# Halves of the FFN operands: powers of two moved into ScalarE's scale, GpSimd's multiplications taken out

## The chip, the cores and the metric

One Trainium2 chip, one of its cores. The time is device microseconds of one execution of the whole kernel; three runs of the kernel before have the median 1286.19 us (1284.73 to 1286.59).

## The reference

Eight sequences of 576 tokens with 8 heads of 64 go through a thresholded attention; its output is a matrix x of 4608 tokens by 512. After it comes the feed-forward part (FFN), the one that the change touches:

```
x = attn_out.transpose(0, 2, 1, 3).reshape(B * S, H * D)     # 4608 x 512
h = x @ w_in                                                 # w_in  512 x 2048
g = np.where(h > 0.0, h, np.exp(np.minimum(h, 0.0)) - 1.0)
out = g @ w_out                                              # w_out 2048 x 512
```

All is float32.

## The kernel before, in words

Most of the program runs attention and the FFN of earlier tokens side by side. There the two FFN products are done block-wise with fewer products (sums of blocks of the weights and tokens are made first, and the partial products are added up again). The last such products, "second_round" of the group before the last two, have their matmuls on L1818, their additions out of PSUM on VectorE at L1827, L1836 and L1838, further additions on GpSimd at L1831, and sums of g at L1765.

The last two groups of 512 tokens, called g7 and g8, are done in another way, which takes the span from 1086 us on (its halves are begun at about 1056 us): each operand is split in two halves of a shorter number format (F32R, which TensorE multiplies in one pass), and three products of halves take the place of one full float32 product. The token plane of 128 x 512 and the weight plane of 128 x 512 each become three planes:

- index 0, the **cut**: the operand times CUT, rounded on writing to F32R (ScalarE, L2004 for tokens, L2024 for weights)
- index 1, the **rest**: operand minus cut (VectorE; tokens at L2008 straight to F32R; weights at L2028 into a float32 slot, after which GpSimd multiplies it by 1/EPS = 4096 into F32R at L2031)
- index 2, the **cross** plane (VectorE; tokens at L2012, in-weights at L2035, out-weights at L2253, once for each token group)

The first round, for each group and each of 16 blocks f of the hidden width (32 units), is 8 matmuls of cut with cut and rest with rest (L2187), a scale by 1 + EPS of the bank in PSUM by ScalarE (L2191), and 4 matmuls of the cross planes two units later (L2200). Then follow exp on ScalarE (L2211), minus 1 on GpSimd (L2214) and the ELU's end on VectorE (L2217), which leaves the raw g block. The second round has, for each group and each f, 12 matmuls (L2264): three for each of four blocks of 128 tokens. EDGE = 3 blocks f at the beginning and at the end of a group are taken together, so that their planes are wanted together.

The order of the work is written by hand. `at(t, job)` puts a job into an agenda at a time of a made-up clock, and `on_pe(cost, job)` first issues all jobs that are due and then moves that clock on by the cost of the matmuls. The times say only in which order instructions go into the queues of the engines; on the chip each engine takes its queue in order and waits for what an instruction needs. A unit costs 2.73 of that clock. `issued(key, x)` pulls the agenda forward when a matmul needs a plane that is not issued yet.

Planes live in slots of 128 x 512. `take` gets one (a float32 or F32R slot that an old tile left, else one from the queue `free`, oldest first), and `drop` gives it back; whoever takes it later waits on the chip for its last reader. The float32 rest of a weight ("d") takes such a slot for a short while. The raw g blocks take float32 slots as well.

Of the kernel before, what the change touches and what calls it, by code (L numbers as in the profile page):

```python
# [10 lines left out]
FP32 = mybir.dt.float32  # L11
U32 = mybir.dt.uint32
I32 = mybir.dt.int32
F32R = mybir.dt.float32r
AF = mybir.ActivationFunctionType
ALU = mybir.AluOpType
# [352 lines left out]
def kernel(  # L369
# [10 lines left out]
    nc = tc.nc  # L380
# [3 lines left out]
    DM, DF = moe_w_in.shape  # L384
# [1230 lines left out]
    with tc.manual_schedule():  # L1615
# [11 lines left out]
        def at(t, f, key=None):  # L1627
            if key and stage[0]:
                t += MOVED.get(stage[0] + key, 0.0)
            serial[0] += 1  # L1630
            heapq.heappush(agenda, (t, serial[0], f))

        def until(t):
            while agenda and agenda[0][0] <= t:
                do_next()
# [333 lines left out]
        EDGE = 3  # L1969
        EPS, CUT = 2.0**-12, 1.0 - 2.0**-13  # L1970
        free, kept_for, parts, split_stack = deque(), {FP32: deque(), F32R: deque()}, {}, ExitStack()
# [9 lines left out]
        def slot(dt, wide=True):  # L1981
            if kept_for[dt]:
                t = kept_for[dt].popleft()
                return t, lambda: kept_for[dt].append(t)
            pool, name = home = free.popleft()
            return pool.tile([P, DM], dt, name=name), lambda: free.append(home)

        def drop(key, *which):
            for x in which or range(len(parts[key])):
                parts[key][x][1]()  # L1990
# [6 lines left out]
        def take(key, dt):  # L1997
            t = slot(dt)
            parts.setdefault(key, []).append(t)
            return t[0]  # L2000

        def cut(key, src, cols=slice(0, DM), fresh=True):
            a = take(key, F32R) if fresh else parts[key][0][0]
            nc.scalar.activation(a[:, cols], src()[:, cols], AF.Copy, scale=CUT)  # L2004

        def rest(key, src, cols=slice(0, DM), fresh=True):
            b = take(key, F32R) if fresh else parts[key][1][0]
            nc.vector.tensor_tensor(b[:, cols], src()[:, cols], parts[key][0][0].bitcast(FP32)[:, cols], ALU.subtract)  # L2008

        def cross(key, src, cols=slice(0, DM), fresh=True):  # L2010
            s = take(key, F32R) if fresh else parts[key][2][0]
            nc.vector.scalar_tensor_tensor(s[:, cols], parts[key][0][0].bitcast(FP32)[:, cols], 1.0 + EPS, src()[:, cols],  # L2012
                                           ALU.mult, ALU.subtract)

        def split_tokens(t, key, src, then=None):
            at(t, lambda: cut(key, src))
            at(t + 0.8, lambda: rest(key, src))
            at(t + 1.5, lambda: (cross(key, src), then and then()))

        def like(t, x):  # L2020
            return t.rearrange("p (j f) -> p j f", f=x.shape[2]) if len(x.shape) == 3 else t

        def weights_cut(key, src):
            nc.scalar.activation(like(take(key, F32R), src()), src(), AF.Copy, scale=CUT)  # L2024

        def weights_rest(key, src):
            d = take(("d", key), FP32)
            nc.vector.tensor_tensor(like(d, src()), src(), like(parts[key][0][0].bitcast(FP32), src()), ALU.subtract)  # L2028

        def weights_scaled(key):  # L2030
            nc.gpsimd.tensor_scalar(take(key, F32R), parts["d", key][0][0], 1.0 / EPS, None, ALU.mult)  # L2031

        def weights_cross(key):
            c, d = (parts[key][x][0].bitcast(FP32) for x in range(2))
            nc.vector.tensor_tensor(take(key, F32R), d, c, ALU.subtract)  # L2035

        def split_weights(t, key, src, then=None):
            at(t, lambda: weights_cut(key, src))
            at(t + 0.7, lambda: (weights_rest(key, src), then and then()))
            at(t + 1.4, lambda: (weights_scaled(key), drop(("d", key))))  # L2040
            if key[0] == "in":
                at(t + 2.1, lambda: weights_cross(key))

        def w_in_of(f):
            return lambda: w_in_at(slice(0, KJ), f * P, P)
# [1 line left out]
        def w_out_of(f):  # L2047
            return lambda: w_out_at(f, slice(0, DM))
# [10 lines left out]
        def x_of(g, j):  # L2059
            return lambda: xts[g][:, j]  # L2060
# [4 lines left out]
        def split_begin():  # L2065
            t = now[0]
            attending[0] = False
            attention.close()
            open_slots("r", 24, "right")
            xts[B] = xpool.tile([P, KJ, MAIN], FP32, name="xt")  # L2070
            nc.sync.dma_start(xts[B][:, : KJ - 1], xtail[: KJ - 1].rearrange("j p n -> p j n"))
            nc.sync.dma_start(xts[B][:, KJ - 1, : late_columns.start], xtail[KJ - 1, :, : late_columns.start])
            for f in range(EARLY_IN):
                at(t + 0.2 + 3.2 * f, lambda f=f: restore_in(f))
                split_weights(t + 0.6 + 3.2 * f, ("in", f), w_in_of(f))
            for j in range(KJ - 1):
                split_tokens(t + 2.2 + 3.2 * j, ("x", B - 1, j), x_of(B - 1, j))
            split_tokens(t + 12.0, ("x", B, 0), x_of(B, 0))
            for f in range(NU, NFT):
                at(t + 11.0 + 1.2 * (f - NU), lambda f=f: restore_in(f))  # L2080
# [3 lines left out]
        for pr in range(JOINED, NP + 2):  # L2084
            t = clock[0]
            b = pr // NPAIR
# [38 lines left out]
        g7, g8, last = B - 1, B, KJ - 1  # L2125
        for t, cols, fresh in ((clock[0] - 0.9, slice(CT, DM), True), (clock[0] + 0.4, slice(0, CT), False)):
            key = ("x", g7, last)
            at(t, lambda cols=cols, fresh=fresh: cut(key, x_of(g7, last), cols, fresh))
            at(t + 0.4, lambda cols=cols, fresh=fresh: rest(key, x_of(g7, last), cols, fresh))
            at(t + 0.8, lambda cols=cols, fresh=fresh: cross(key, x_of(g7, last), cols, fresh))  # L2130
        until(clock[0] + 0.3)
        run_extra(99)
        strassen.close()
# [22 lines left out]
        for j, t in ((1, 0.9), (2, 4.6), (last, 7.4)):  # L2156
            split_tokens(begin + t, ("x", g8, j), x_of(g8, j),
                         (lambda: [give(xpool, "xt", FP32) for _ in range(2)]) if j == last else None)
# [5 lines left out]
        def out_done(f):  # L2164
            if f % 4 == 3:
                give(const, f"w_out{f // 4}", F32R)

        for f in range(EARLY_IN, NFT):
            t = max(begin + 0.4 + 3.4 * (f - EARLY_IN), start_of[g7, f] - LEAD)
            if f < NU:  # L2170
                at(t - 0.5, lambda f=f: restore_in(f))
            split_weights(t, ("in", f), w_in_of(f), lambda f=f: in_done(f))
# [62 lines left out]
        def g_of(g, f):  # L2235
            def src():
                while (g, f) not in raw_g:
                    do_next()
                return raw_g[g, f]

            return src

        def start_f(t0, f):
            return t0 if f < EDGE else min(t0 + UNIT * f, t0 + UNIT * (NFT - EDGE))

        OUT_EARLY = 11
        for f in range(NFT):
            split_weights(begin + 22.0 + 3.9 * f if f < OUT_EARLY else start_f(middle, f) - 9.0, ("out", f), w_out_of(f),
                          lambda f=f: out_done(f))
            for g, t0 in ((g7, middle), (g8, end)):  # L2250
                t = start_f(t0, f) - (9.5 if f < EDGE else 6.0) + 2.9 * f * (f < EDGE)
                split_tokens(t, ("h", g, f), g_of(g, f), lambda g=g, f=f: drop(("g", g, f)))
                at(t + 2.2, lambda g=g, f=f: nc.vector.tensor_tensor(  # L2253
                    take(("cross", g, f), F32R), parts["out", f][1][0].bitcast(FP32), parts["out", f][0][0].bitcast(FP32),
                    ALU.subtract))

        left = {(g, f): 4 for g in (g7, g8) for f in range(NFT)}

# [79 lines left out]
```

## Time and profile before

| | |
|---|---|
| median of 3 runs | 1286.19 us |
| the profiled execution's own time | 1286.68 us |
| its span, first to last instruction | 1284.9 us |
| TensorE busy, matmuls | 1253.4 us (98% of the span) |
| VectorE / ScalarE / GpSimd busy | 1039.1 / 635.6 / 784.4 us |
| mean granted TensorE clock | 0.995 |
| first matmul of the first round (L2187) | at 1086.47 us of the span |
| first matmul of the second round (L2264) | at 1188.93 us |
| last matmul | ends by 1280.13 us |

How to read the profile: PE is TensorE's matmuls, PEld its weight loads, DVE VectorE, ACT ScalarE, POOL GpSimd. A group is "line engine operation out<-in": busy time, mean of one, then the idle time of the engine before it and what ended that ("<-"). In the table of stretches each engine has its busy time and number of instructions, then come the granted clock (1.00 is full) and the DMA engines' share. In the list in order of time a row is start, duration, engine, line, and in square brackets how long the engine had been idle and for whom. The tile names in it are those of memory that was used before under that name, since slots are handed on: "l" and "r" are the two pools of slots.

### The profile page before, as it was taken

To read this page: it belongs to the slowest core of one execution; us is meant where nothing else is said; L and a number is where in the kernel's file an instruction comes from. 1 tells how busy PE (TensorE), PEld (TensorE's weight loads), DVE (VectorE), ACT (ScalarE), POOL (GpSimd) and SP (SyncE) were. 2 spreads that over 40 slices of the span, in tenths; PEclk is the share of its full clock that TensorE was granted. 3 is DMA by queue.
4 is the path that set the end of the run, shared out by engine and by line. 5 is a ranking of instruction groups with operands and counts; after the bars stand their busy time and mean duration, and the time that the engine had idled before them with its cause. 6 is when DMAs were issued, how large, how long until landed. Compare 5 with 4: busy or idle time off the path is not lost. (4 is left out here: it accounts for less than half of the span.)

```text
span 1284.9 us, 21199 instructions
## 1 busy us (share of the span) xinstructions
PE 1253.4 (98%) x6598; PEld 959.7 (75%) x6598; DVE 1039.1 (81%) x2199; ACT 635.6 (49%) x1331; POOL 784.4 (61%) x1093
## 2 busy tenths in 40 slices
PE   8999999999999999999999999999999998989998
PEld 6675575467778887878788888788788886767876
DVE  6888877878889979898889888988899767645775
ACT  7899775664443535252625353434435342535322
POOL 4778655776586747684767567665767463575110
PEclk9999999999999999999999999999999999989999
DMA  7566689998989988999889898989899871000001
GB/s 139 150 171 189 172 235 250 259 255 201 243 228 237 251 238 228 266 246 233 239 230 260 221 257 223 252 232 237 221 243 244 257 220 56 1 1 1 1 33 33
DMA packets 325551, 245.74 MB, mean 191 GB/s; under 512 B 209216, under 2 KB 289984, under 8 KB 325440
## 3 DMA queue, kind: packets, MB, share of 16 engines
q1 hardware_dynamic: 323264, 243.65, 70.7%
q8 instruction: 52, 0.85, 0.3%
q10 hardware_dynamic: 2176, 0.75, 0.2%
q14 instruction: 59, 0.48, 0.1%
HBM read 154.53 MB, written 89.78 MB: 190 GB/s over the span
## 5 line engine op out<-in xcount | busy, mean ns | idle before, releaser
L984 DVE TENSOR_REDUCE mx<-sc 128x1 f32<-128x576 f32 x207 | 148.3, 750 | 29.8 <-PE sc L977 25.8
L726 POOL TENSOR_SCALAR w<-w,rs 128x576 f32<-128x576 f32 x144 | 116.3, 816 | 70.5 <-DVE rs L789 69.9
L1004 ACT ACTIVATE w<-sc,mx 128x576 f32<-128x576 f32 x113 | 81.5, 740 | 115.0 <-DVE mx L984 98.0
L868 DVE STREAM_TRANSPOSE x<-w 128x512 f32<-128x512 f32 (+1 forms) x153 | 108.9, 744 | 15.1 <-POOL w L726 11.3
L996 POOL TENSOR_SCALAR th<-mx,ntau 128x2 f32<-128x2 f32 (+1 forms) x114 | 34.0, 298 | 133.4 <-DVE mx L984 133.4
L977 PE MATMUL sc<-kT,qT 64*128 64x448 f32 (+4 forms) x736 | 102.8, 416 | 0.0
L977 PEld LDWEIGHTS sc<-kT,qT 64*128 64x128 f32 x736 | 81.0, 186 | 24.3 <-issue 16.2
L1011 DVE SCALAR_TENSOR_TENSOR w<-sc,th,w 128x576 f32<-128x576 f32 x113 | 88.2, 810 | 9.5 <-ACT w L1004 9.2
L1678 PE MATMUL f<-xt,sw 128*128 128x256 f32 x384 | 93.8, 387 | 1.0 <-ACT g L1740 0.5
L1818 PE MATMUL f<-w_out,s 128*128 128x256 f32 x384 | 92.1, 383 | 2.1 <-DVE ot L1836 1.6
L1818 PE MATMUL f<-t,s 128*128 128x256 f32 x384 | 91.2, 380 | 2.8 <-DVE ot L1836 1.9
L1678 PE MATMUL f<-xt,w_in 128*128 128x256 f32 x384 | 91.8, 382 | 0.5 <-ACT w L1692 0.5
L1818 PE MATMUL f<-w_out,g 128*128 128x256 f32 x384 | 92.0, 382 | 0.0
L1678 PE MATMUL f<-x,w_in 128*128 128x256 f32 x384 | 90.8, 379 | 0.0
L726 POOL TENSOR_SCALAR e<-e,rs 128x576 f32<-128x576 f32 x91 | 67.3, 743 | 35.2 <-DVE rs L789 33.8
L1818 PEld LDWEIGHTS f<-t,s 128*128 128x128 f32 x384 | 72.7, 190 | 13.7 <-DVE ot L1836 2.3
L1818 PEld LDWEIGHTS f<-w_out,s 128*128 128x128 f32 x384 | 71.8, 190 | 14.8 <-issue 2.5
L1678 PEld LDWEIGHTS f<-xt,sw 128*128 128x128 f32 x384 | 69.3, 189 | 18.0 <-issue 5.5
L1818 PEld LDWEIGHTS f<-w_out,g 128*128 128x128 f32 x384 | 72.0, 190 | 12.5 <-issue 3.2
L1678 PEld LDWEIGHTS f<-xt,w_in 128*128 128x128 f32 x384 | 72.0, 190 | 12.5 <-ACT w L1692 2.7
L1678 PEld LDWEIGHTS f<-x,w_in 128*128 128x128 f32 x384 | 72.9, 190 | 10.1 <-ACT s L1692 0.3
L1765 POOL TENSOR_TENSOR s<-g 128x256 f32<-128x256 f32 x96 | 75.4, 790 | 7.9 <-DVE g L1728 7.4
(369 smaller groups left out, 3176.4 us busy)
## 6 DMA issues: line engine op xcount, KB each, us to landing
there<-x SPq DMA_DIRECT2D x444, 144.0 KB, 3.6
wTb<-there SPq DMA_DIRECT2D x58, 576.0 KB, 6.4
wTa<-there SPq DMA_DIRECT2D x53, 576.0 KB, 5.1
sw<-win_sums SPq DMA_DIRECT2D x46, 384.0 KB, 4.8
t<-wout_sums SPq DMA_DIRECT2D x33, 512.0 KB, 6.2
qm<-in_q_dram SPq DMA_DIRECT2D x124, 72.0 KB, 5.0
wst<-in_moe_w_in_dram SPq DMA_DIRECT2D x16, 512.0 KB, 4.2
vm<-in_v_dram SPq DMA_DIRECT2D x64, 128.0 KB, 3.6
```

The source lines that it names most:

```text
L726: nc.gpsimd.tensor_scalar(wv, wv, st["rs"][:, h : h + 1], 1.0, ALU.mult, ALU.mult)
L868: nc.vector.transpose(x[:, :, c0 : c0 + nc_], src.rearrange("p (c g n) -> p g c n", c=nc_, n=T))
L977: on_banks(nc.tensor.matmul(o, qT[r, i * P : (i + 1) * P], kT[r, k0 : k0 + n], start=True, stop=True, skip_group_check=True), o)
L984: on_banks(nc.vector.tensor_reduce(st["mx"][:, h : h + 1], st["sc", h], axis=AX.XY if i == NC else AX.X, op=ALU.max, negate=True), st["sc" ...
L996: nc.gpsimd.tensor_scalar(st["th"][:, cs], st["mx"][:, cs], -1.0, ntau, ALU.mult, ALU.add)
L1004: on_banks(nc.scalar.activation(st["e", h], st["sc", h], AF.Exp, bias=st["mx"][:, h : h + 1]), st["sc", h])
L1011: on_banks(nc.vector.scalar_tensor_tensor(st["e", h], st["sc", h], st["th"][:, h : h + 1], st["e", h], ALU.is_ge, ALU.mult, accum_out=st[" ...
L1678: nc.tensor.matmul(loc["banks"][place], left[:, j], right[:, j], start=(begins and j == 0), stop=(j == 1), skip_group_check=True)
L1765: engine.tensor_tensor(o, x, y, op)
L1818: nc.tensor.matmul(place(m), lhs, rhs, start=(begins and v == 0), stop=(v == RU - 1), skip_group_check=True)
```

## The change

The tokens' cut takes in 1/EPS (scale CUT / EPS), and the weights' cut takes in EPS (scale CUT * EPS), so that the products keep their size. The tokens' rest becomes operand times 1/EPS minus the cut, one scalar_tensor_tensor instead of one tensor_tensor. The tokens' cross becomes cut times EPS minus the rest; it no longer reads the operand but the rest, so `then` (which gives back the raw g slot) moves from behind the cross to behind the rest. The weights' rest becomes cut times -1/EPS plus the operand, one scalar_tensor_tensor that writes the F32R plane directly; GpSimd's multiplication and the float32 slot are gone. The cross of the in-weights is put at t + 1.4 where it stood at t + 2.1. The cross of the out-weights is the same subtraction, through the same helper. The tokens of the first three blocks f of each group in the second round are split at 11.5 - 3.2 f ahead of the round's start, instead of 9.5 - 2.9 f.

```diff
         def cut(key, src, cols=slice(0, DM), fresh=True):
             a = take(key, F32R) if fresh else parts[key][0][0]
-            nc.scalar.activation(a[:, cols], src()[:, cols], AF.Copy, scale=CUT)
+            nc.scalar.activation(a[:, cols], src()[:, cols], AF.Copy, scale=CUT / EPS)
 
         def rest(key, src, cols=slice(0, DM), fresh=True):
             b = take(key, F32R) if fresh else parts[key][1][0]
-            nc.vector.tensor_tensor(b[:, cols], src()[:, cols], parts[key][0][0].bitcast(FP32)[:, cols], ALU.subtract)
-
-        def cross(key, src, cols=slice(0, DM), fresh=True):
+            nc.vector.scalar_tensor_tensor(b[:, cols], src()[:, cols], 1.0 / EPS, parts[key][0][0].bitcast(FP32)[:, cols],
+                                           ALU.mult, ALU.subtract)
+
+        def cross(key, cols=slice(0, DM), fresh=True):
             s = take(key, F32R) if fresh else parts[key][2][0]
-            nc.vector.scalar_tensor_tensor(s[:, cols], parts[key][0][0].bitcast(FP32)[:, cols], 1.0 + EPS, src()[:, cols],
-                                           ALU.mult, ALU.subtract)
+            a, b = (parts[key][x][0].bitcast(FP32)[:, cols] for x in range(2))
+            nc.vector.scalar_tensor_tensor(s[:, cols], a, EPS, b, ALU.mult, ALU.subtract)
 
         def split_tokens(t, key, src, then=None):
             at(t, lambda: cut(key, src))
-            at(t + 0.8, lambda: rest(key, src))
-            at(t + 1.5, lambda: (cross(key, src), then and then()))
+            at(t + 0.8, lambda: (rest(key, src), then and then()))
+            at(t + 1.5, lambda: cross(key))
...
         def weights_cut(key, src):
-            nc.scalar.activation(like(take(key, F32R), src()), src(), AF.Copy, scale=CUT)
+            nc.scalar.activation(like(take(key, F32R), src()), src(), AF.Copy, scale=CUT * EPS)
 
         def weights_rest(key, src):
-            d = take(("d", key), FP32)
-            nc.vector.tensor_tensor(like(d, src()), src(), like(parts[key][0][0].bitcast(FP32), src()), ALU.subtract)
-
-        def weights_scaled(key):
-            nc.gpsimd.tensor_scalar(take(key, F32R), parts["d", key][0][0], 1.0 / EPS, None, ALU.mult)
-
-        def weights_cross(key):
+            c = parts[key][0][0].bitcast(FP32)
+            nc.vector.scalar_tensor_tensor(like(take(key, F32R), src()), like(c, src()), -1.0 / EPS, src(), ALU.mult, ALU.add)
+
+        def weights_cross(key, into):
             c, d = (parts[key][x][0].bitcast(FP32) for x in range(2))
-            nc.vector.tensor_tensor(take(key, F32R), d, c, ALU.subtract)
+            nc.vector.tensor_tensor(take(into, F32R), d, c, ALU.subtract)
 
         def split_weights(t, key, src, then=None):
             at(t, lambda: weights_cut(key, src))
             at(t + 0.7, lambda: (weights_rest(key, src), then and then()))
-            at(t + 1.4, lambda: (weights_scaled(key), drop(("d", key))))
             if key[0] == "in":
-                at(t + 2.1, lambda: weights_cross(key))
+                at(t + 1.4, lambda: weights_cross(key, key))
...
             for g, t0 in ((g7, middle), (g8, end)):
-                t = start_f(t0, f) - (9.5 if f < EDGE else 6.0) + 2.9 * f * (f < EDGE)
+                t = start_f(t0, f) - (11.5 if f < EDGE else 6.0) + 3.2 * f * (f < EDGE)
                 split_tokens(t, ("h", g, f), g_of(g, f), lambda g=g, f=f: drop(("g", g, f)))
-                at(t + 2.2, lambda g=g, f=f: nc.vector.tensor_tensor(
-                    take(("cross", g, f), F32R), parts["out", f][1][0].bitcast(FP32), parts["out", f][0][0].bitcast(FP32),
-                    ALU.subtract))
+                at(t + 2.2, lambda g=g, f=f: weights_cross(("out", f), ("cross", g, f)))
```

More of the change, by code (lines that the diff above doesn't have):

```diff
@@ L2129 @@
             at(t + 0.4, lambda cols=cols, fresh=fresh: rest(key, x_of(g7, last), cols, fresh))
-            at(t + 0.8, lambda cols=cols, fresh=fresh: cross(key, x_of(g7, last), cols, fresh))
+            at(t + 0.8, lambda cols=cols, fresh=fresh: cross(key, cols, fresh))
         until(clock[0] + 0.3)
```

## The prediction

> **What bounds the kernel now.** First the table of stretches, in pieces of 4 us from 1084 us on (busy time of PE, PEld, DVE, ACT, POOL, then granted clock, DMA share, GB/s): where is TensorE short of 4.00?
>
> ```profile
> 1116.00:1120.00 4.00, 4.00 (x19) 3.16 (x18) 2.37 (x4) 2.25 (x5) 3.84 (x3) 1.00 0.00 0
> 1120.00:1124.00 4.00, 3.37 (x15) 2.44 (x13) 2.23 (x4) 1.83 (x4) 2.18 (x3) 1.00 0.00 0
> 1124.00:1128.00 4.00, 1.70 (x4) 1.42 (x5) 1.21 (x2) 0.00 (x0) 3.84 (x4) 0.79 0.02 4
> 1128.00:1132.00 4.00, 4.00 (x15) 3.22 (x15) 2.74 (x6) 2.64 (x5) 2.76 (x3) 0.78 0.00 0
> ...
> 1148.00:1152.00 4.00, 3.27 (x11) 2.63 (x12) 1.98 (x3) 2.49 (x6) 2.52 (x3) 0.78 0.00 0
> ```
>
> When TensorE runs dry, GpSimd alone is full (3.84 of 4); behind two of the gaps the clock is below 0.8, with 15 and 11 matmuls in 4 us instead of 19. Next the waits, of TensorE alone, from 1050 us to the end (total us, times, longest):
>
> ```profile
> PE f L2187 <- POOL l L2031: 7.7, 3, 2.9
> PE f L1818 <- DVE ot L1836: 3.5, 2, 1.9
> PE f L2187 <- POOL r L2031: 1.7, 1, 1.7
> PE f L2264 <- DVE l L2253: 1.2, 1, 1.2
> PE f L1818 <- POOL s L1765: 0.9, 1, 0.9
> PE f L2187 <- POOL w_out L2031: 0.7, 1, 0.7
> PE f L1818 <- DVE s L1765: 0.5, 1, 0.5
> PE f L1818 <- DVE ot L1838: 0.4, 1, 0.4
> ```
>
> L2031 is the multiplication that the change removes. It ends five waits of the first round (7.7 + 1.7 + 0.7 = 10.1 us). The rest is 5.3 us ahead of that round (L1818) and 1.2 us in the second. Last, the list in order of time before the longest wait:
>
> ```profile
> 1121.10 0.69 DVE L2217 SCALAR_TENSOR_TENSOR xt<-xt,f 128x512 f32<-128x512 f32 x1 [1.58 <-POOL xt L2214]
> ...
> 1122.64 0.68 DVE L2028 TENSOR_TENSOR w_in<-w_in,l 128x512 f32<-128x512 f32 x1
> 1122.76 0.19 PEld L2187 LDWEIGHTS f<-r,l 128*128 128x128 f32 x1
> 1122.81 1.87 POOL L2031 TENSOR_SCALAR l<-xt 128x512 fp32r<-128x512 f32 x1 [1.74 <-DVE xt L2028]
> 1122.98 0.39 PE L2187 MATMUL f<-r,l 128*128 128x512 f32 x1
> 1124.76 1.49 POOL L2031 TENSOR_SCALAR l<-w_in 128x512 fp32r<-128x512 f32 x1
> 1126.28 0.69 DVE L2035 TENSOR_TENSOR l<-l,l 128x512 fp32r<-128x512 f32 x1 [2.95 <-POOL l L2031]
> 1126.30 2.64 PEld L2187 LDWEIGHTS f<-r,l 128*128 128x128 f32 x7 [3.35 <-POOL l L2031]
> 1126.30 3.35 PE L2187 MATMUL f<-r,l 128*128 128x512 f32 x7 [2.93 <-POOL l L2031]
> ```
>
> The in-weights' plain rest is ready at 1123.3, but its multiplication waits behind that of out-weights which nobody needs for 60 us. VectorE's next entry, the cross plane at 1126.28, waits for the same plane and blocks the ELU behind it. The cut had been made at 1117.23: ScalarE is not late. VectorE's rest itself was late because L2217 waited for GpSimd's L2214, again behind L2031. So it is GpSimd's queue, not TensorE's sum of work, that ends the waits that matter here, although the page's busy share (98% TensorE) doesn't show it.
>
> **The change, part by part.** All durations are of 128 x 512 planes from the groups between 1050 us and the end.
>
> 1. *ScalarE's cuts* keep count and form (about 0.62 each); another constant in the scale costs nothing that a row would show.
>
> 2. *VectorE's instructions* keep their number. Tensor_tensor (L2008, L2028) becomes scalar_tensor_tensor; L2012 is that form with the same types already, and both have means of 0.68 to 0.69 us where GpSimd is quiet. Difference 0, bounds -0.01 to +0.01 us each. What can cost is that the cross now reads what the instruction just ahead of it wrote. Independent neighbours start 0.61 us apart though they last 0.69 (L2008 at 1203.95, L2012 at 1204.56); the pair L783, L789, which depends, starts 0.03 us behind the first's end (1038.25 + 0.16 to 1038.44). So a dependent pair loses 0.08 + 0.03 = 0.11 us, where nothing stands between the two; bounds 0 and 0.11, and I take 0.11.
>
> 3. *GpSimd's multiplications*, 32 of 1.49 us at least (the page's list of L2031 has 1.49 to 1.87), go: 48 us of that queue. Each also slows VectorE where it starts. Between 1212 and 1224 us five VectorE instructions last 1.09 to 1.14 instead of 0.68, each overlapping an L2031.
>
> 4. *The first round* runs from 1086.47 to 1188.93, 102.5 us. An undisturbed unit takes 2.72 us (L2187 at 1092.74, next at 1095.46), 32 of them 87.0. The excess is 15.4: the 10.1 of waits; the slow clock behind two of them, where 11 matmuls from 1126.30 to 1130.51 take 4.21 instead of 11 x 0.227 = 2.5 and 20 from 1148.73 to 1154.79 take 6.06 instead of 4.5, together 3.2; and 2.1 of restarts and small waits. What is late next? VectorE is: its 97 instructions there take 58.8 us, and it waits 16.6 us for GpSimd's minus 1 (L2214), 75 of 87. ScalarE's 50 us and GpSimd's 24.5 (L2214 alone) are farther off. I leave 1.5 us of excess: the round takes 88.5, gain 13.9. Bounds of the gain: 15.4, and 7 if VectorE holds it (a rival below).
>
> 5. *Ahead of the first round* (1060 to 1082 us) TensorE waits 1.88 + 1.59 + 0.35 + 0.55 = 4.4 us for VectorE and 0.9 for GpSimd. In the same stretch VectorE stands still three times for L2031 (1.40, 1.02, 1.27 = 3.7 us, each ahead of L2035). With those gone, less three pairs of 0.11, VectorE comes 3.4 us earlier; GpSimd's L1831 and L1765 no longer queue behind the multiplication at 1070.25 to 1071.74, which covers its 0.9. Gain 4.3, bounds 2 (half of VectorE's time is refilled by additions that wait for TensorE itself) and 5.3 (all).
>
> 6. *Second round.* Its one wait, 1.2 us at 1226, is for the cross planes of blocks 13 to 15, when VectorE has been full since 1212. The five slowed instructions of point 3 cost it 5 x 0.42 = 2.1 us; two or three dependent pairs give 0.3 back. 1.8 is more than 1.2, so the wait goes: gain 1.2, bounds 0 and 1.3. Moving the first three blocks' splits 2.0, 1.7 and 1.4 earlier adds no instruction; for g8 they stand at clock 32.2 of the g7 half, behind the last cross planes at 31.7, so nothing urgent queues behind them. Behind a cut that waits for a slot stand ScalarE's scale and exp; a scale is wanted two units (5.4 us) later, which hides waits of that size (the longest for a slot of TensorE's there is 5.5). Bounds 0 and 1 us.
>
> Sum: 4.3 + 13.9 + 1.2 = 19.4 us. The profiled execution took 1286.68 (span 1284.9, 1.8 around it), so 1267.3 by its own time; the median is 0.5 lower, 1266.8. I say 1267.0.
>
> One rule speaks otherwise. Row first: after waits of 2.93 and 2.19 us matmuls came about 0.42 to 0.48 us apart instead of 0.227; after 2.57 and 1.66 us they did not. The Trainium skill (TensorE: Matmul & The Clock Gate, "HAM oscillation — how this bites in real kernels") puts the fall to half rate at idle gaps beyond about 3.4 us. By that, no wait here would cost clock, the 3.2 us would be something else and stay, and the time would be 1270.2; the granted clock of 0.78 just there is against it, so the trace decides.
>
> **Rivals.**
>
> *A, VectorE takes GpSimd's place.* Where out-weights are made beside the first round (some 14 units), its work per unit of 2.72 us is: ELU 0.61 and its wait of 0.51; half an in-weight's rest, cross and restore 0.8; 0.43 of an out-weight's rest; 0.32 of restore_out: 2.67. Half a dependent pair makes 2.72. If GpSimd's minus slows one instruction per unit (restore_out 0.83 instead of 0.42 at 1104.52), 14 units run over by 0.35, 4.9 us, and gaps like the two above add 3.2 of slow clock: gain 11.3, 1275. For: the waits of L2217. Against: the lead of 8 clock units of each weight, and the whole round's 75 of 87.
>
> *B, the multiplication isn't what binds*: the planes stay late for slots or for the order of the queues, and only points 5's 0.9, 6 and half the clock loss come: 0.9 + 1.2 + 1.6 = 3.7, 1283. For: ScalarE's exp waits for slots (L2211, 17 us). Against: nearly all of those waits are for L2031, too.
>
> *C, slower: VectorE's instruction that makes a plane costs more than its row.* Price: 1.13 us each instead of 0.61 from start to start, as in the slowed rows. First round: 14 units with 1.7 such instructions, 2.67 + 1.7 x 0.52 = 3.55, 14 x 0.83 = 11.7 us over. Second: 3 per unit, 3.39 against TensorE's 2.81 (12 matmuls 0.234 apart), 32 x 0.58 = 18.6. Together 30.3 less the gain of 19.4: 1297 to 1298. It decides from where 23.8 (p - 0.61) + 32 (3p - 2.81) reaches 19.4, p = 1.04 us. For: such durations exist. Against: they stand beside GpSimd's starts, which become fewer, and L2012 has the form and 0.68.
>
> **How the numbers follow.** Forecast 0.68, A 0.19, B 0.06, C 0.05, no change within 0.2% (2.6 us, about what a measurement can tell) 0.02. The forecast's own bounds: all gains in full give 5.3 + 15.4 + 1.3 = 22.0, 1264.7; low gains of points 5 and 6 (2 and 0, less 1) with 13.9 give 1271.8. The range runs from 1264.5 to 1276, forecast and most of A, 0.68 + 0.16. Faster 0.68 + 0.19 + 0.06 = 0.93, same 0.02, slower 0.05.
>
> **What would show it.** TensorE's waits of L2187 for L2031 gone, with no wait over 1 us in their place; the first round 88 to 89 us, its clock 1.00 throughout; GpSimd's busy time 48 us or more lower; VectorE's three idle pieces before the in-weights' cross near 1060 to 1072 gone and the first round beginning 4 us earlier; L2264 without a wait at the end of g7. Wrong would be waits for VectorE's rest or ELU, or for ScalarE's cut (slots), of the same size.

## The result, and the profile after

The changed kernel takes 1264.24 us (median of 4 runs, 1263.22 to 1264.56) beside 1286.09 of the kernel before: ratio 0.983, interval 0.9813 to 0.9847. Forecast were 1267.0 us and a range from 1264.5; the direction was right, the gain of 21.9 us a little larger than the 19.4 of the sum and 0.26 us past the range's end. The profiled execution took 1264.46 us with a span of 1262.7; that of before 1286.68 and 1284.9. One execution of the kernel before, in a later comparison, took 3282.55 us and is left out of every figure.

First the same table of stretches as before, of the kernel after (PE, PEld, DVE, ACT, POOL busy; granted clock; DMA):

```profile
1120.00:1124.00 4.00, 4.00 (x19) 3.29 (x18) 2.83 (x6) 2.65 (x5) 0.68 (x2) 1.00 0.00 0
1124.00:1128.00 4.00, 4.00 (x20) 3.27 (x19) 3.08 (x5) 2.44 (x5) 1.28 (x2) 1.00 0.00 0
1128.00:1132.00 4.00, 4.00 (x19) 3.31 (x18) 2.89 (x4) 2.47 (x5) 0.97 (x2) 1.00 0.01 2
1148.00:1152.00 4.00, 4.00 (x19) 3.29 (x18) 2.24 (x3) 1.65 (x4) 1.26 (x2) 1.00 0.00 0
```

TensorE is full in each, with 19 or 20 matmuls per 4 us and clock 1.00; GpSimd, at 3.84 before, does about 1 us of work. Over the whole span its busy time fell from 784.4 to 728.9 us. TensorE's waits from 1040 us to the end, all of them:

```profile
PE f L1818 <- DVE ot L1836: 1.0, 1, 1.0
PE f L1818 <- DVE s L1765: 0.5, 1, 0.5
PE f L1818 <- POOL s L1765: 0.3, 1, 0.3
```

The 10.1 us of waits in the first round and the 1.2 of the second are gone. 3.5 us ahead of the first round have gone too, and 1.8 are left.

Where the 22.2 us between the two spans lie, from the first matmul of each round and the last one:

| stretch | before | after | gain | forecast |
|---|---|---|---|---|
| up to the first restore of w_in (the first work of the halves) | 1055.9 | 1054.2 | 1.7 | 0 |
| from there to the first round's first matmul | 30.6 | 26.4 | 4.2 | 4.3 |
| first round | 102.7 | 87.9 | 14.8 | 13.9 |
| second round, to the start of its last matmul | 90.5 | 88.8 | 1.7 | 1.2 |
| rest | 5.2 | 5.4 | -0.2 | 0 |

The first row lies ahead of everything that the change touches. It comes from the stretch near 260 us. Before, then after:

```profile
256.00:259.00 3.00, 1.22 (x4) 0.30 (x2) 2.94 (x5) 2.02 (x4) 2.86 (x6) 1.00 0.96 301
259.00:263.00 4.00, 4.00 (x21) 1.98 (x22) 1.94 (x4) 1.71 (x6) 4.00 (x5) 0.57 0.59 120
```

```profile
256.00:259.00 3.00, 0.95 (x4) 0.30 (x2) 2.91 (x6) 2.02 (x4) 2.86 (x6) 1.00 0.92 296
259.00:263.00 4.00, 4.00 (x30) 2.23 (x29) 2.52 (x5) 2.27 (x6) 4.00 (x5) 1.00 0.61 130
```

Both have the same idle TensorE at 257 us (a wait of 1.8 and of 2.0 us at L925). Behind it the clock fell to 0.57 in the execution before, and did not in the one after: 21 matmuls in 4 us against 30. Matmul by matmul, the execution before is 0.2 us behind the other at 242 us of the span and 1.5 behind at 282; small gains and losses elsewhere make the 1.7.

### The profile page after: what moved, and what is told of

Its sections match the earlier page's. It is cut to its first block, busy times and chain, and to the rows that moved or that the text cites. A ratio compares the mean times of both kernels' runs of the same rounds, so it can differ in the third digit from the quotient of the medians.

```text
span 1262.7 us, 21127 instructions
## 1 busy us (share of the span) xinstructions
PE 1245.7 (99%) x6598; PEld 956.6 (76%) x6598; DVE 1041.7 (83%) x2199; ACT 636.6 (50%) x1331; POOL 728.9 (58%) x1061
## 4 chain that ended last, share of the span: by engine, by line
PE 90%; DVE 4%; POOL 2%; DMA 1%; issue 1%; ACT 1%; SPq 0%; DVEq 0%; ACTq 0%; POOLq 0%
PE f L1818 22%; PE f L1678 22%; PE sc L977 8%; PE sc L1050 7%; PE f L2259 6%; PE f L2184 5%; PE f L1102 4%; PE sc L673 3%; PE f L1154 3%; PE f L2197 2%; PE pv L930 2%; PE rt L792 1%; PE sc L1042 1%; PE sc L1037 1%; DVE x L868 1%
## 5 line engine op out<-in xcount | busy, mean ns | idle before, releaser
L977 PE MATMUL sc<-kT,qT 64*128 64x448 f32 (+4 forms) x736 | 102.7, 416 | 0.0
L1678 PEld LDWEIGHTS f<-x,w_in 128*128 128x128 f32 x384 | 72.9, 190 | 10.1 <-ACT s L1692 0.3
L1765 POOL TENSOR_TENSOR s<-g 128x256 f32<-128x256 f32 x96 | 75.1, 788 | 7.9 <-DVE g L1728 7.4
```

The source lines that it names most:

```text
L977: on_banks(nc.tensor.matmul(o, qT[r, i * P : (i + 1) * P], kT[r, k0 : k0 + n], start=True, stop=True, skip_group_check=True), o)
L1678: nc.tensor.matmul(loc["banks"][place], left[:, j], right[:, j], start=(begins and j == 0), stop=(j == 1), skip_group_check=True)
L1765: engine.tensor_tensor(o, x, y, op)
```

## The experiments

The time before in each comparison is that of runs on the same chip, taken together with it (medians 1285.3 to 1286.1 us). "First round" is the time from its first matmul to the first of the second round, in the profiled execution.

### Which part of the change does it

**The weights' part alone.** The tokens' helpers and the early splits are as before, the weights' as after, so the output has another scale and only the time is of use.

```diff
 # kernel after
-            nc.scalar.activation(a[:, cols], src()[:, cols], AF.Copy, scale=CUT / EPS)
+            nc.scalar.activation(a[:, cols], src()[:, cols], AF.Copy, scale=CUT)
...
-                t = start_f(t0, f) - (11.5 if f < EDGE else 6.0) + 3.2 * f * (f < EDGE)
+                t = start_f(t0, f) - (9.5 if f < EDGE else 6.0) + 2.9 * f * (f < EDGE)
```

> The weights' planes as after (ScalarE's scale takes in EPS, VectorE writes the rest, no GpSimd multiplication), the tokens' planes and the early splits of the first three blocks as before. The powers of two of the two sides then do not cancel, so this kernel computes the products at another scale; the instructions are the same. Theory (GpSimd's multiplication binds): nearly all of the gain, 20 to 22 us under the kernel before; first round about 88 us, no wait for L2031's place. Rival (the tokens' new form, with the raw block given back earlier, or the earlier splits carry a part): 10 to 17 us under.

Measured 1264.29 us (1263.33 to 1265.24), ratio 0.983 (0.9816 to 0.9843); first round 87.9; TensorE's waits are line for line those of the kernel after. So the weights' part carries the whole gain.

**The tokens' part alone**, on the kernel before:

```diff
-            nc.vector.tensor_tensor(b[:, cols], src()[:, cols], parts[key][0][0].bitcast(FP32)[:, cols], ALU.subtract)
+            nc.vector.scalar_tensor_tensor(b[:, cols], src()[:, cols], 1.0, parts[key][0][0].bitcast(FP32)[:, cols],
+                                           ALU.mult, ALU.subtract)
...
+            nc.vector.scalar_tensor_tensor(s[:, cols], a, EPS, b, ALU.mult, ALU.subtract)
```

> The tokens' instructions in their new form (rest by scalar_tensor_tensor, cross from cut and rest, raw block given back behind the rest), with factor 1 instead of the power of two, and the weights with GpSimd's multiplication as before. Theory: within 1.5 us of the kernel before, the waits of L2187 for L2031 all there; VectorE 0.11 us later per pair of rest and cross that stand next to each other, some 2 us in its whole queue and none on the path. Rival (the tokens' form matters): 3 to 8 us faster, or, if the dependent pair costs more than its row, 2 to 5 us slower.

Measured 1286.05 us, ratio 1.0005 (0.9995 to 1.0014). The waits are the old ones:

```profile
PE f L2188 <- POOL l L2032: 7.6, 3, 2.9
PE f L1818 <- DVE ot L1836: 3.5, 2, 1.9
PE f L2188 <- POOL r L2032: 1.8, 1, 1.8
PE f L2265 <- DVE l L2254: 1.5, 1, 1.5
```

L2032 and L2188 are L2031 and L2187, one line lower here. The wait in the second round is 0.3 longer, and no more comes of the new dependence.

**The early splits alone**, and **taken back**:

```diff
 # kernel before (and the reverse in the kernel after)
-                t = start_f(t0, f) - (9.5 if f < EDGE else 6.0) + 2.9 * f * (f < EDGE)
+                t = start_f(t0, f) - (11.5 if f < EDGE else 6.0) + 3.2 * f * (f < EDGE)
```

> The kernel before with nothing changed but the start of the first three blocks' token splits (11.5 - 3.2 f ahead instead of 9.5 - 2.9 f). Theory: no change, within 1.5 us, and the 1.2 us wait of the second round at the end of g7 stays or grows by less than 1 us. Rival (the earlier splits carry a part of the gain): 1 to 3 us faster.

> The changed kernel with the first three blocks' token splits back at 9.5 - 2.9 f ahead. Theory: the earlier splits only fill idle time, so within 0.8 us of the changed kernel, about 1264.5 us. Rival: the beginning of g7's or g8's second half waits for the planes of block 0 to 2, 1 to 3 us more than the changed kernel.

Measured 1285.89 us on the kernel before, ratio 0.9998 (0.9989 to 1.0007), and 1263.79 us on the kernel after (5 runs, 1263.63 to 1265.51), as near to the changed kernel's 1264.24 as its own runs. They do nothing that can be measured here.

### Is it the extra pass, or GpSimd?

The multiplication stays in the chain of cut, rest and cross, but another engine makes it (edits to the kernel before):

```diff
-            nc.gpsimd.tensor_scalar(take(key, F32R), parts["d", key][0][0], 1.0 / EPS, None, ALU.mult)
+            nc.scalar.activation(take(key, F32R), parts["d", key][0][0], AF.Copy, scale=1.0 / EPS)
 # or
+            nc.vector.tensor_scalar(take(key, F32R), parts["d", key][0][0], 1.0 / EPS, None, ALU.mult)
```

> The kernel before, but the multiplication of the weights' rest by 4096 is made by ScalarE (an activation with that scale, at the same place of the order, same planes and slots) and not by GpSimd. Theory (the wait for GpSimd's queue is what costs, not the extra pass as such): ScalarE's 50 us in the first round become 65 of 87, each pass 0.62 instead of 1.49 us, so 16 to 21 us faster than the kernel before, at most 4 us behind the changed kernel. Rival (one pass more in the chain of cut, rest, cross makes the planes late wherever it runs): at most 8 us faster than before.

> The kernel before, but the multiplication is made by VectorE. Theory: no plane waits for another engine any more, but VectorE has 32 instructions more, of 0.4 to 0.7 us each; in the first round 58.8 us of work become 70 to 76, with its waits for minus 1 near the 87 that TensorE needs: 12 to 20 us faster than the kernel before, with some waits of TensorE for VectorE left. Rival (VectorE's share is the bound next): at most 8 us faster, waits of over 1 us for VectorE in every second unit.

On ScalarE 1265.63 us, ratio 0.9848 (0.9832 to 0.9863); on VectorE 1266.93 us, 0.9857 (0.9842 to 0.9873). Both have a first round of 87.8 us, as good as without the pass. VectorE is busy for 71.0 of those 87.8 and holds nobody up in them. So one pass more on another engine leaves the kernel 1.4 to 2.7 us behind the kernel after (ahead of the first round 0.9 and 1.3 us, in the second round 0.5 and 1.3), and the rest comes with GpSimd's instruction. Whether with the engine or with the instruction's own 1.49 us, these two kernels can't tell; the last experiment does.

### What a busy GpSimd does

Here the kernel after gets a multiplication back that nobody reads, with the old one's size, types and place in the order:

```diff
+        def spare(key):
+            nc.gpsimd.tensor_scalar(take(("z", key), F32R), parts[key][1][0].bitcast(FP32), 1.0, None, ALU.mult)
+            drop(("z", key))
...
             at(t + 0.7, lambda: (weights_rest(key, src), then and then()))
+            at(t + 1.4, lambda: spare(key))
```

> The changed kernel plus a GpSimd multiplication for each weight plane (same size and types as the one that went, at the same place of the order) whose result goes to a slot of its own and is read by nobody. GpSimd's queue is then as full as before, but no matmul and no cross plane waits for it. Theory (planes' wait for the queue costs most; VectorE's waits for minus 1 and the slower VectorE instructions beside GpSimd cost a little): 1 to 5 us slower than the changed kernel, so 16 to 20 us faster than before. Rival 1 (a busy GpSimd costs through shared memory access and through minus 1 in its queue, whoever waits for the plane): over 10 us slower than the changed kernel. Rival 2: not slower at all, within 0.8 us.

Measured 1277.68 us, 13.4 more than the kernel after, as rival 1 had it. The first theory (the planes' own wait) falls here as the whole cause: no plane comes from GpSimd, and yet the first round takes 94.8 us, 7 of the 14.8 that the change had won there, and the matmuls wait for planes, now named after VectorE (the four largest of TensorE's waits, then VectorE's two largest between 1080 and 1180 us):

```profile
PE f L2264 <- DVE r L2033: 2.3, 1, 2.3
PE f L2189 <- DVE l L2029: 2.1, 2, 1.7
PE f L2189 <- DVE w_out L2029: 1.8, 2, 1.7
PE f L2264 <- DVE w_out L2033: 1.8, 1, 1.8
```

```profile
DVE w_in L2219 <- POOL w_in L2216: 17.5, 12, 2.4
DVE xt L2219 <- POOL xt L2216: 8.2, 6, 2.4
```

L2216 is minus 1, L2219 the ELU's end behind it. In the kernel after, VectorE waits for minus 1 at most 2.1 us at a time and some 13 us in all of the first round (6.0 + 3.7 + 1.6 + 1.5). The list in order of time shows how:

```profile
1112.08 1.49 POOL L2036 TENSOR_SCALAR l<-l 128x512 fp32r<-128x512 f32 x1
1113.54 0.61 POOL L2216 TENSOR_SCALAR xt<-xt 128x512 f32<-128x512 f32 x1
1114.18 0.69 DVE L2219 SCALAR_TENSOR_TENSOR xt<-xt,f 128x512 f32<-128x512 f32 x1 [1.35 <-POOL xt L2216]
1115.12 0.69 DVE L2029 SCALAR_TENSOR_TENSOR r<-l,w_out 128x512 fp32r<-128x512 f32 x1
1115.73 0.69 DVE L2029 SCALAR_TENSOR_TENSOR r<-l,w_in 128x512 fp32r<-128x512 f32 x1
```

The spare multiplication (L2036) holds minus 1 for 1.49 us, VectorE stands still at the ELU, and the rests of the weights (L2029), which need nothing from GpSimd, stand behind it in VectorE's queue.

The second round takes 94.7 us, more than in the kernel before (90.5), so that part of the loss belongs to the spare multiplication and not to the old one.

New theory: minus 1 behind the multiplication is one way; slots are another, since a slot that GpSimd wrote is handed on and its next owner waits (in the second round ScalarE waits 6.4 us once for L2036). Three kernels tell the ways apart: minus 1 moved to ScalarE, the spare result in a tile of its own, and both.

```diff
-                nc.gpsimd.tensor_scalar(loc["h"], loc["h"], 1.0, -1.0, ALU.mult, ALU.add)
+                nc.scalar.activation(loc["h"], loc["h"], AF.Copy, bias=-1.0)
 # and / or
-            nc.gpsimd.tensor_scalar(take(("z", key), F32R), parts[key][1][0].bitcast(FP32), 1.0, None, ALU.mult)
-            drop(("z", key))
+            nc.gpsimd.tensor_scalar(private["z"], parts[key][1][0].bitcast(FP32), 1.0, None, ALU.mult)
```

> The changed kernel with the spare GpSimd multiplication, and minus 1 of the ELU moved from GpSimd to ScalarE. Theory now (the multiplication costs because minus 1 stands behind it, VectorE's ELU waits for that, and the weights' rests stand behind the ELU): the loss of 13.4 us falls to 5 or less, since nothing that VectorE waits for is left in GpSimd's queue; ScalarE's 51 us in the first round become 70 of 87. Rival 1 (the loss comes from slots that wait for GpSimd): 6 to 13 us slower than the changed kernel still. Rival 2 (shared access to memory): the same.

> The changed kernel with the spare GpSimd multiplication from the first round on, its result going to a tile of its own (in bfloat16, for room) and not to one of the slots that ScalarE and VectorE take next. Minus 1 stays on GpSimd. Theory (minus 1 behind the multiplication): still 8 to 14 us slower than the changed kernel. Rival (slots): 0 to 4 us slower.

> Both: the spare multiplication into a tile of its own, and minus 1 on ScalarE. What is left is a busy GpSimd that nobody waits for, apart from the slots of the rests that it reads. Theory: 0 to 2 us slower than the changed kernel. Rival (shared access to memory slows VectorE by itself): 5 us or more slower, with VectorE's instructions beside GpSimd's at 1.1 us instead of 0.68.

| spare multiplication, kernel after | time, us | first round | second round |
|---|---|---|---|
| none | 1264.24 | 87.9 | 88.8 |
| into a slot, minus 1 on GpSimd | 1277.68 | 94.8 | 94.7 |
| into a slot, minus 1 on ScalarE | 1272.72 | 87.9 | 94.7 |
| into its own tile, minus 1 on GpSimd | 1272.77 | 94.9 | 90.4 |
| into its own tile, minus 1 on ScalarE | 1265.02 | 87.9 | 89.9 |

The two ways are separate and each has its stage. Minus 1 in the same queue costs the first round 7 us, whatever the slots; the slots cost the second round 4 to 5 us, whatever minus 1. With both gone, a GpSimd that is busy for 40.6 us of the first round costs that round nothing and the kernel 0.8 us, no more than the comparisons differ among themselves; in its profile the second round is 1.1 us longer. (The kernels with a tile of its own begin the spare work with the first round, three blocks later; that is 1.0 us ahead of the round, 26.4 instead of 27.4.) The theory written ahead of these three kernels, minus 1 alone, was wrong for half of the loss.

### The kernel before once more

Does the same hold for the kernel before, where the cross planes and matmuls do wait for the multiplication? Minus 1 goes to ScalarE there, and, as a control, in the kernel after; the edit is the first one above.

> The kernel before, with minus 1 of the ELU moved from GpSimd to ScalarE; GpSimd keeps the multiplications, and the cross planes and matmuls still wait for them. If minus 1 in the same queue is what costs: first round 88 to 90 us instead of 102.5, 12 to 16 us faster than the kernel before. If the planes' own wait for 1.49 us multiplications costs (the step as predicted): first round 95 us or more, at most 8 us faster. Both: in between.

> The changed kernel with minus 1 on ScalarE, as the control for the kernels with minus 1 moved. ScalarE's work in the first round rises from 52 to about 71 of 88 us. Expected: within 1.5 us of the changed kernel, first round 88 us. If ScalarE's order holds something up: 2 to 4 us slower.

The kernel before becomes 1270.36 us, ratio 0.9884 (0.9868 to 0.9901), its first round 88.7 us instead of 102.7, with the multiplications and all that reads them in place. TensorE's only wait there:

```profile
PE f L2187 <- POOL l L2031: 0.3, 1, 0.3
```

It was 10.1. VectorE's cross planes still wait for L2031 (in the same profile, from 1040 us on; 3.7 of the 5.1 us lie ahead of the round):

```profile
DVE l L2035 <- POOL l L2031: 12.5, 6, 3.0
DVE r L2035 <- POOL r L2031: 5.1, 4, 1.4
DVE l L2035 <- POOL w_out L2031: 2.3, 2, 1.9
```

Inside the first round these waits come to 19.3 us, beside 20.9 in the kernel before, so they hardly changed, although GpSimd has less work there (38.8 instead of 62.3 us); what is left of them costs the round 0.8 us. Ahead of the first round nothing changed (30.6 us, as before), since minus 1 of the halves isn't there yet. The control: 1264.78 us, first round 87.9.

### The size of the multiplication

Every multiplication so far took 1.49 us alone, minus 1 of the same size 0.62. First the output type, on the kernel with the spare one:

```diff
-            nc.gpsimd.tensor_scalar(take(("z", key), F32R), parts[key][1][0].bitcast(FP32), 1.0, None, ALU.mult)
+            nc.gpsimd.tensor_scalar(take(("z", key), FP32), parts[key][1][0].bitcast(FP32), 1.0, None, ALU.mult)
```

> As the kernel with the spare multiplication, but the result goes to a float32 slot. Theory: GpSimd's 1.49 us for a 128 x 512 multiplication come from the F32R output (minus 1, with two operations and float32 output, takes 0.62 us alone), so 0.6 to 0.8 us each here and half or less of the other's loss, under 2 us slower than the changed kernel. Rival: 1.49 us again, as the operation itself takes so long.

1272.91 us, but not for the reason expected: the instruction keeps its size with a float32 output, and what fell is the second round (90.0 us). That fits the slots, since `take` hands on float32 slots of old tiles apart from the F32R ones that the cuts take; it was not tested further. The time is 8.7 us over the kernel after, and the first round stays at 94.1:

```profile
L2036 POOL TENSOR_SCALAR w_in<-l x10: 1484/1622/1991, 1085.8 to 1210.8; 128x512 f32<-128x512 f32 x10
```

Then the form. On the kernel before, a second operation that changes nothing:

```diff
-            nc.gpsimd.tensor_scalar(take(key, F32R), parts["d", key][0][0], 1.0 / EPS, None, ALU.mult)
+            nc.gpsimd.tensor_scalar(take(key, F32R), parts["d", key][0][0], 1.0 / EPS, 0.0, ALU.mult, ALU.add)
```

> The kernel before, with GpSimd's multiplication of the weights' rest written with a second operation that changes nothing (times 4096, plus 0). In every profile so far the multiplication with one operation takes 1.49 us, with F32R and with float32 output, while minus 1 (times 1, plus -1) takes 0.62. Theory (the one-operation form is the slow one): 0.62 to 0.9 us each, GpSimd's queue 25 us shorter, and most of the waits for L2031 go: 12 to 19 us faster than the kernel before. Rival (the size belongs to something else, in place or not, or the first operand): 1.49 us again and no change, within 1.5 us.

1267.81 us, ratio 0.9867 (0.9844 to 0.989). Two of the instruction's rows (ns, least/median/most) and TensorE's waits from 1040 us on:

```profile
L2031 POOL TENSOR_SCALAR l<-w_in x4: 619/620/900, 1094.1 to 1145.4; 128x512 fp32r<-128x512 f32 x4
L2031 POOL TENSOR_SCALAR r<-r x3: 617/619/721, 1059.8 to 1068.1; 128x512 fp32r<-128x512 f32 x3
```

```profile
PE f L1818 <- DVE ot L1836: 1.7, 2, 1.0
PE f L2264 <- DVE l L2253: 1.2, 1, 1.2
PE f L1818 <- DVE s L1765: 0.5, 1, 0.5
PE f L1818 <- DVE ot L1838: 0.4, 1, 0.4
```

The first round is 87.7 us and has no wait, though GpSimd makes all 32 products. One operand more brings 17 of the 22 us that the change brings. It is the whole gain of the first round (15.0 us) and 2.6 of the 4.2 ahead of it; the second round keeps its 90.6 us.

## Why the prediction was right or wrong, point by point

**What binds: half right.** GpSimd's queue and the multiplication in it were the cause, and the sum of work said nothing of it. But the step "It ends five waits of the first round" took the name in TensorE's row for the cause. Alone, the plane's own wait costs the first round 0.8 us (before_minus_act). The other way, named in the same paragraph as why VectorE's rest was late, costs 7 of the 14.8 us alone (after_spare): multiplication, minus 1 behind it, VectorE at the ELU, the next rests behind that. The other 7 are there only when both ways are, as in the kernel before; how they divide was not measured. The price came near because both ways end with the same instruction, which is luck as far as the path goes.

**Points 1 and 2, ScalarE and VectorE: right for the cuts (0.62 to 0.63 us) and the rests**, which have 0.68 to 0.69 us in the new form. Of a dependent pair standing next to each other, after:

```profile
1057.65 0.68 DVE L2029 SCALAR_TENSOR_TENSOR r<-r,w_in 128x512 fp32r<-128x512 f32 x1
1058.37 1.10 DVE L2033 TENSOR_TENSOR r<-r,r 128x512 fp32r<-128x512 f32 x1
```

0.72 from start to start, 0.11 more than independent ones, as worked out; in the whole kernel it doesn't show (tokens_form).

**Point 3: right in the price, wrong in what it may cost.** VectorE's instructions beside a GpSimd start are still slowed (1.10 above, beside GpSimd's L1831). The point overlooked that the cross of the in-weights, which no longer waits for GpSimd, now runs beside minus 1: 12 of them in the first round take 0.91 to 1.10 us instead of 0.69, and VectorE is busy for 62.9 us there instead of 59.0. It has room for it, as TensorE waits for nothing in that round; with the spare multiplications running as well, in spare_private_minus_act, the kernel loses 0.8 us.

**Point 4, first round: mis-sized.** I left 1.5 us above the ideal 87.0, with no row for it; it was 0.9. With the 102.7 of this reckoning the gain is 14.8, not 13.9. The 3.2 us of slow clock went with the waits, and the stretches are at 1.00. In the other executions with the old first round it was much the same: 102.8 and 104.0 us.

**Point 5, ahead of the first round: right**, 4.2 us against 4.3; weights_only has the same 26.4, tokens_form the old 30.5.

**Point 6, second round: mis-sized.** 1.7 against 1.2; the wait is 1.2 of it, and 0.5 I have not traced. The early splits do nothing, as said.

**The sum: the step that failed is "so 1267.3 by its own time", and with it the low end of the range.** The sum put everything outside its three stages at nothing, as if only the change could alter the profiled execution. The three stages gave 4.2 + 14.8 + 1.7 = 20.7 us instead of 19.4 (0.9 and 0.5 too little in points 4 and 6, 0.1 too much in point 5). The stretch ahead of them gave 1.7 more, most of it the slow clock at 260 us, and the rest after the last matmul took 0.2 back: 22.2 between the spans. Between the medians it is 21.9, so about 1.2 us come from outside the stages there, if these gained the same; how much of that is slow clock can't be told, since only one execution of each kernel was profiled.

The range has a slip besides. Its low end takes the 22.0 us of all gains in full from the profiled 1286.68 (1264.7, put at 1264.5), while the forecast itself had gone over to the median, 0.5 lower. Taken from that median of 1286.19, the same gains end at 1264.2, and 1264.24 was measured.

The slow clock is not tied to the change. In 16 profiled executions of these kernels the idle TensorE at 257 us (1.6 to 2.9 us) is followed by it in 7 (before, weights_only, before_act_mult, after_spare_f32, before_two_ops, spare_minus_act, after_minus_act) and not in 9. The traces' records of the granted clock show what decides. From 30 us of the span to the last matmul the clock falls 18 times in the 16 executions, for 3.41 us each time (twice 6.83), and each fall comes a whole number of such steps after the clock first became full: 74 steps, 252.6 us, in all 7 at 260 us. In the step just ahead of a fall TensorE is idle for 1.78 to 2.93 us. No step with 1.76 us or less is followed by one; of those with more, one isn't (before_new_edges, 1.81 us at 257 us). So a gap costs clock when enough of it lies in one step. In the execution before, the gap at 257 us lies whole in a step; in the one after, a longer gap is cut in two at 257.6 us (before, then after, each step with the one behind it):

```profile
255.90:259.30 3.40, 1.62 (x6) 0.49 (x7) 3.28 (x6) 2.39 (x5) 3.26 (x6) 1.00 0.91 287
259.30:262.70 3.40, 3.40 (x18) 1.61 (x18) 1.68 (x3) 1.14 (x4) 3.40 (x5) 0.51 0.57 117
```

```profile
254.20:257.60 3.40, 2.38 (x10) 1.06 (x6) 3.21 (x9) 2.71 (x6) 2.81 (x6) 1.00 0.96 293
257.60:261.00 3.40, 2.37 (x18) 1.36 (x18) 3.04 (x6) 1.90 (x4) 3.40 (x4) 1.00 0.69 198
```

It also answers why, in the first round before, the waits of 2.93 and 2.19 us cost clock and that of 2.57 did not: 2.93 and 1.93 us of them lie in one step, and the third is cut into 1.31 and 1.26.

The Trainium skill (TensorE: Matmul & The Clock Gate, "What's actually happening") has the window over which TensorE's activity is judged run freely, so that the same gap can meet it at another place each time. These steps agree. Its length of about 3.4 us of idle time doesn't: here 1.78 us idle within one step were enough.

**Rivals.** A: refuted by before_dve_mult, whose VectorE has 71.0 us of work in a first round of 87.8 without a wait. My working for A added up a dense stretch as if it were steady: in the kernel after VectorE reaches 3.62 of 4 us once (1104 to 1108 us), and 2.86 on average in the first round. B: weights_only alone can't refute it, as it changes slots and order too; before_two_ops does, with the old slots and order, a shorter instruction and a first round of 87.7 us. C: refuted by the time and the rests' 0.69; the slowed crosses of point 3 are near its price and hold nobody up.

The remaining 1.8 us of TensorE's waits ahead of the first round (VectorE's additions at L1836 and L1765) were not tried: they are 0.14% of the time, less than these runs can tell.

## What to carry to other kernels

A wait's named releaser is the last link of a chain and need not be its cause: look what stood ahead of it in the releaser's own queue, and what stands behind the instruction that waits. An optional piece of work on an engine can cost through its order (short urgent work behind it, slots that it hands on) and not through its share; here 29 such instructions cost 0.8 us once nothing urgent shares their queue or slots. Before work is moved off an engine, measure the instruction itself in its other forms.

## What the runs showed of the hardware that was not expected

Where nothing disturbs it, GpSimd's tensor_scalar on 128 x 512 float32 takes 1.49 us with one operation (times 4096) and 0.62 us with two (times 4096, then plus 0), with the same input and F32R output; the one-operation form has 1.48 to 1.49 us with float32 and bfloat16 outputs as well. It isn't the number of operations as such: minimum with 1, then plus -1 (L1124, float32 in place) takes 1.92 us in the kernel before. Why isn't known from these runs.

VectorE's tensor_scalar with one operation, same sizes, takes 0.41 to 0.47 us where nothing disturbs it, less than the 0.69 of its two-tensor instructions (before_dve_mult).

The granted clock falls on a grid of 3.41 us that each execution begins anew, after 1.78 us or more of idle TensorE within one step (18 falls in 16 traces, with one step of 1.81 us that was not followed by a fall).
